# A two-column exponential bias, w_mod ahead of x, one more head group by seven products, another feed-forward order and a search over orders, in an adaLN transformer block

## The chip, the core and the metric

The kernel runs on one core of one Trainium2 chip. The metric is the device time of one execution in microseconds. A core has five engines that each follow an instruction queue of their own: PE (TensorE, matmuls), DVE (VectorE), ACT (ScalarE), POOL (GpSimd) and SP (SyncE, which issues the DMAs here). Engines wait for each other through semaphores. PE writes to PSUM, which has eight banks of 128 x 512 f32; the other tiles lie in SBUF.

## What is computed

```python
def _A_ref(x, k_cache, v_cache, wq, wo):            # 2048 queries, 32 heads of 128, window W = 512 keys
    q = (x @ wq).reshape(B, Sq, Hq, Dh).transpose(0, 2, 1, 3)
    k, v = k_cache[:, :, Sk - W:, :], v_cache[:, :, Sk - W:, :]
    p = softmax(einsum("bhqd,bhkd->bhqk", q, k) * Dh ** -0.5)
    o = einsum("bhqk,bhkd->bhqd", p, v)
    return o.transpose(0, 2, 1, 3).reshape(B, Sq, Hq * Dh) @ wo

def _B_ref(x, w_gate, w_up, w_down):                # Dm 512, Df 1376
    return (gelu(x @ w_gate) * (x @ w_up)) @ w_down

mod = (silu(c) @ w_mod).reshape(1, 6, 1, 512)
sa, ca, ga, sb, cb, gb = (mod[:, i] for i in range(6))
x = x + ga * _A_ref(layernorm(x) * (1 + ca) + sa, ...)
x = x + gb * _B_ref(layernorm(x) * (1 + cb) + sb, ...)
```

Inputs and output are f32.

## The kernel before

**Numbers.** A product of f32 matrices is done with f16 pairs: each operand is split into a high part and the low rest, and three f16 matmuls (high-high, high-low, low-high) add up in one PSUM bank. Names of tiles in the trace: `acc` (16 tiles of 128 x 512) is x and then the residual; `raw` a weight or cache tile as loaded; `A`, `B`, `T`, `S` the split operands of the q product; `k` and `kT` the keys and their transposes; `q`; `p` the exponentials in f32; `pp` their f16 pair; `pT` its transposes by DMA; `oT` the attention output; `st` a small tile with a query block's maxima, biases and sums; `es` a head's scale; `psQ`, `psS`, `psW`, `psO` PSUM banks.

**Attention.** 128 iterations (`NIT`): 16 groups of two heads, each over four query groups of 512. An iteration has two halves, each for 256 queries: PE makes scores into a pair of banks psS (two pairs in turn), DVE takes the row maximum (`s_max`, `st<-psS`), turns it into the bias of the exponential (`st<-st,es`), ACT does two exponentials with that bias (`s_exp`), ACT copies the high part and POOL subtracts for the low part (`pp<-p,pp`), SP transposes both by DMA. Two iterations later PE multiplies by v into psO (one bank), ACT and DVE split the result to oT; three iterations later PE multiplies by wo into psW (two banks) and DVE adds into acc. The next iterations' q goes through psQ (one bank), and ACT and DVE split it. Beside this run the preparations of the next head group (maxima on DVE, scaling and splitting of raw tiles on ACT and POOL), spread over half iterations by `STEPS`.

**q by seven products.** The q products of two heads and two query groups, with the model dimension in two halves, are a 2 x 2 product of blocks. From head group `WINO` on they are made as Strassen and Winograd do: seven products of sums in place of eight (42 matmuls in place of 48), twice for a head group. This needs sums T1 to T4 of h, made once (`t_full`, `t_sum`, `t_split`, on POOL, ACT and DVE), and sums S1 to S4 of each group's weights.

**Feed-forward.** 11 blocks of 128 hidden columns (the last of 96), two halves p of the queries. A unit (p, f) is a block for one half; from block `PLAIN` = 2 on it is made by seven products too (`product`, `stage`), four stages with ACT and DVE behind each (`r`, `hid`), and a queue of down products (`down_put`, `down`) is worked off one after each stage. `UNITS` is the order of the units. `aw_load` and `aw_make` prepare the weights of a later unit; `SPLIT` lists the units that need it (blocks 6 to 9 share their weights between p = 0 and p = 1). The second half's sums (`sums_a`, `sums_b`) are issued at block 4 of the first half.

**Order.** Nothing is issued where it is written. `Weaver` notes every operation with its readers and writers (`note`), ranks the operations back from the end (`rank`), and `issue` plays the program forward against a model of the engines (`play`) and back (`back`), in turns; the best of 8 turns (`TURNS`) is kept up to a point of time, and so on for the points in `CUTS`. Then each engine gets its instructions in the planned order, all from line 418 of the profile. In the plan an operation that `note` marks as `lock` cannot run beside one of POOL: all of POOL's operations, and DVE's tensor_scalar and two-operand operations on SBUF tiles, where they have more than two columns. Where POOL's operation follows closely behind such a one of DVE, an extra wait is put in ("POOL lets DVE in"). The loads ahead of `nc.lead` are issued as written.

**Start.** `PLAN` lists the first steps by name ("stats", "mod", "row", "col" and so on); `mod` is silu(c) @ w_mod for the rows sa and ca (`wm`, four tiles each), and its bound decides the scale of h.

Of the kernel before, what the change touches and what calls it, by code (L numbers as in the profile page):

```python
# [2 lines left out]

# [10 lines left out]
OP = mybir.AluOpType  # L14
# [14 lines left out]
NF = (DFF + P - 1) // P  # L29
# [9 lines left out]
HID = 2.0 ** 38  # L39
HQS = 2.0 ** 9  # L40
QDOWN = 2.0 ** -16
WINO = 3
GATED = 12
ODOWN = 2.0 ** -22
ROUND = 1.0 + 2.0 ** -7
# [34 lines left out]
)  # L80

EARLY = {("wq", 0): (0, 3, 9, 10), ("wq", 1): (0, 3, 10, 11), ("k", 0): (0, 6, 9, 11, 12), ("k", 1): (0, 4, 11, 13, 15),
         ("v", 0): (3, 7, 13, 14), ("wo", 0): (4, 10, 13, 17), ("v", 1): (6, 8, 15, 20), ("wo", 1): (7, 11, 19, 22)}
EARLY_CROSS = (7, 9)
# [2 lines left out]
class Weaver:  # L87
# [1 line left out]

    LAG, DRAIN, LANES, TURNS, SPAN, SHY, EARLY, WORTH = 60.0, 165.0, 8, 8, 3413.0, 1500.0, 40000.0, 5000.0  # L90
    NEAR = 1000.0
    CUTS, BEYOND = (130000.0, 700000.0, 1280000.0, 1400000.0, 1500000.0, None), 25000.0
    NEXT = {"ACT": 95.0, "DVE": 85.0, "POOL": 45.0, "PE": 0.0, "SP": 0.0}

    def __init__(self, nc, tc):
        self.nc, self.tc = nc, tc
        for name, engine in (("vector", "DVE"), ("scalar", "ACT"), ("gpsimd", "POOL"), ("tensor", "PE"), ("sync", "SP")):
            setattr(self, name, self.Port(self, engine, getattr(nc, name)))
        self.joins, self.lead = None, 0
        self.ops, self.held, self.seen, self.before, self.rings, self.table = [], {}, {}, {}, {}, {}  # L100

    class Port:
# [61 lines left out]
    def note(self, engine, what, real, a, k):  # L164
        op = len(self.ops) - bool(self.joins)
        wrote = [x for x in (a[0] if a else k["out"], k.get("accum_out")) if x is not None]
        read = [x for x in list(a[1:]) + list(k.values()) if hasattr(x, "ap") and x is not k.get("accum_out")]
        deps = set()
        n = 1
        for x, write in [(x, False) for x in read] + [(x, True) for x in wrote]:  # L170
            m, lo, hi = self.extent(x)
            n = max(n, m) if engine != "PE" else self.extent(wrote[0])[0]
            key = x.name
            held = self.held.get(key)
            if held is None or write and self.joins:
                continue
            alone = held[:1] == [None]
            if alone:
                lo, hi = -1, 1 << 30
            for e in held:  # L180
                if e and (write or e[3] or alone and self.ops[e[2]][0] != engine) and e[0] < hi and lo < e[1]:
                    deps.add(e[2])
            if write:
                held[:] = [e for e in held if not e or not (lo <= e[0] and e[1] <= hi)]
            held.append((lo, hi, op, write))
            self.seen[key].add(op)
        if what == "activation" and a[2] not in (AF.Copy, AF.Identity):
            for f, s in self.table.items():
                if f != a[2]:
                    deps |= s  # L190
            self.table.setdefault(a[2], set()).add(op)
        deps.discard(op)
        d = (470.0 if what == "dma_start" else 1290.0) if engine == "SP" else self.cost(engine, what, a, k, n, [x.name for x in read])
        if engine == "SP":
            short = what == "dma_start" and any(len(x.ap) > 2 and list(x.ap)[-1][1] <= P for x in a[:2])
            n = 1450.0 if what != "dma_start" else n * 4 * P / (195.0 if short else 390.0)
        flat = [x for x in read if self.extent(x)[0] > 1]
        lock = engine == "POOL" or (engine == "DVE" and not any(x.name.startswith("ps") for x in flat) and n > 2 and
                                    (what == "tensor_scalar" or (len(flat) == 2 and what != "tensor_reduce")))
        if self.joins:  # L200
            self.ops[op][2].update(deps)
        else:
            self.ops.append((engine, d, deps, n, {}))
        self.ops[op][4][engine] = d, lock, real, a, k
# [184 lines left out]
    def done(self, ends, by, until):  # L389

        return sum(1.0 if ends[n] < until else 0.0 for n, e in enumerate(by) if e == "PE" and self.ops[n][3] == N)

    def issue(self):
        at, users = self.rank()
        span, keep, cut = None, {}, 0.0
        for stop in self.CUTS:
            best = None
            for _ in range(self.TURNS):
                order, ends, by, starts = self.play(at, users, span, keep, cut)
                span = max(ends)  # L400
                mark = self.done(ends, by, stop + self.BEYOND) if stop else -span
                if best is None or mark > best[0]:
                    best = mark, order, ends, by, starts
                at = self.back(ends, by, users)
            _, order, ends, by, starts = best
            span = max(ends)
            at = self.back(ends, by, users)
            if stop:
                keep, cut = {n: (starts[n], by[n]) for n in order if starts[n] < stop}, stop
        yields, last = {}, None  # L410
        for n in sorted((n for n in order if self.ops[n][4][by[n]][1]), key=lambda n: starts[n]):
            if by[n] == "POOL" and last is not None and starts[n] < ends[last] + self.NEAR:
                yields[n] = last
            last = n if by[n] == "DVE" else None
        made = {}
        for n in order:
            real, a, k = self.ops[n][4][by[n]][2:]
            made[n] = real(*a, **k)  # L418
            if n in yields:
                self.tc.add_manual_dep(made[n].ins, made[yields[n]].ins.name,  # L420
                                       mybir.DependencyInfo(mybir.DependencyClass.Sync, mybir.DependencyReason.DATA),
                                       reason="POOL lets DVE in")
# [3 lines left out]
def adaln_block(ctx: ExitStack, tc: tile.TileContext, x, k_cache, v_cache, wq, wo,  # L426
# [16 lines left out]
    def small(pool, cols_, bufs=3, name="sm"):  # L443
        return pool.tile([P, cols_], F32, name=name, tag=name, bufs=bufs)
# [116 lines left out]
    def load_mod(j):  # L561
        wm[j] = right.tile([P, NC, D], F32, name="wm", tag="pT", bufs=3)
        for k in range(NC):
            nc.sync.dma_start(wm[j][:, k, :], wmod_r[:, k, j * D:(j + 1) * D])

    def load_x(qg):
        for t in range(4 * qg, 4 * qg + 4):
            nc.sync.dma_start(acc[t], x[t * P:(t + 1) * P, :])
# [4 lines left out]
    def load_raw(kind, h):  # L573
# [9 lines left out]
            nc.sync.dma_start(t, wo[h * DH:(h + 1) * DH, :])  # L583
        RAW[kind, h] = t

    load_x(0)
    load_x(1)
    load_mod(1)
    load_mod(0)
    load_raw("k", 0)  # L590
    load_raw("wq", 0)
    load_x(2)
    load_raw("wq", 1)
    load_raw("k", 1)
    load_x(3)
    load_raw("v", 0)
    load_raw("wo", 0)
    load_raw("v", 1)
    load_raw("wo", 1)
    nc.lead = len(nc.ops)  # L600


    e = small(base, NC, 1, "sil")
    nc.scalar.activation(e, csb, AF.Exp, scale=-1.0)
    nc.vector.tensor_scalar_add(e, e, 1.0)
# [2 lines left out]
    spread = right.tile([P, NC, D], F32, name="spread", tag="pT", bufs=3)  # L608
    for k in range(NC):
        nc.vector.tensor_scalar_mul(spread[:, 0, k * P:(k + 1) * P], ones, silu[:, k:k + 1])  # L610


    KINDS = ("wq", "k", "v", "wo")
# [218 lines left out]
    def s_max(it, b):  # L832
        if b == 0:
            ST[it] = small(right, 12, 5, "st")
        st = ST[it]
        nc.vector.tensor_reduce(st[:, 2 * b:2 * b + 2], PSS[it, b], op=OP.max, axis=AX.X, negate=True)
        for n in (2 * b, 2 * b + 1):
            nc.vector.tensor_scalar(st[:, n:n + 1], st[:, n:n + 1], ES[head_qg(it)[0]][:, 0:1], LOG_PS,
                                    op0=OP.mult, op1=OP.add)

    def s_exp(it, b):
        st = ST[it]
# [174 lines left out]
    for half, name, *a in PLAN:  # L1017
        if name == "chunk":
            a[3:] = [ENG[e] for e in a[3:]]
        if half < 0:  # L1020
            STEP[name](*a)
        else:
            at(half, STEP[name], *a)

# [33 lines left out]

    for p in range(2):
        for c in range(2):  # L1060
            n = 8 + 7 * (2 * p + c)
            at(n, t_full, p, c, "11", Y)
            at(n, t_full, p, c, "12", Y)
            at(n + 1, t_sum, p, c, "11", "12", "11")
# [368 lines left out]
    def aw_load(u):  # L1433
        ff_load(u[1], u)
# [166 lines left out]
    for c, (a, b, d) in enumerate(((15.5, 15, 16.25), (15, 16.25, 16.5), (16.5, 16, 17.25), (16, 17.25, 17.5))):  # L1601
        at(e + a, ln2_chunk, 0, c)
        at(e + b, ln2_high, 0, c)
        at(e + d, ln2_low, 0, c, nc.gpsimd)
    UNITS = [(0, f) for f in range(PLAIN, 6)] + [(p, f) for f in range(6, NF - 1) for p in range(2)] + \
        [(0, NF - 1)] + [(1, f) for f in range(6)] + [(1, NF - 1)]
    SPLIT = [u for u in UNITS if not (u[0] and 6 <= u[1] < NF - 1)]
    at(e + 10, aw_load, UNITS[0])
    at(e + 11, aw_load, UNITS[1])
# [81 lines left out]
    for n, u in enumerate(UNITS):  # L1691
        p, f = u
        k = SPLIT.index(u) if u in SPLIT else None
        if k is not None:
            if k + 4 < len(SPLIT):
                aw_load(SPLIT[k + 4])
            if k + 2 < len(SPLIT):
                aw_make(SPLIT[k + 2])
        if WDS:
            w = WDS.pop(0)  # L1700
            wd_load(w)
# [58 lines left out]
```

## Time and profile before

| | us |
|---|---|
| median of 3 runs | 1678.78 (1678.69 to 1679.83) |
| the profiled execution | 1676.12 |
| its span in the trace | 1674.3 |
| first f16 matmul | 26.42 |
| first scores, first product with v | 31.96, 52.01 |
| last matmul ends | 1669.9 |

The profiled execution is one of its own; the trace gives its span, and the 1.8 us between span and time lie around it. All instructions of the weave have line 418 (L418), so a row is told by its engine and its tiles: `DVE TENSOR_SCALAR st<-st,es` is the bias. In a row of the timeline the two numbers ahead are the start and the length in us, and the square brackets hold the idle time before it and what ended that. In a row of the grouped view the numbers behind the first bar are the busy time in us and the mean of one in ns, behind the second the idle time before. The granted TensorE clock was 0.998 of full speed on the mean.

### The profile page before, as it was taken

The page shows a single profiled execution, that of the slowest core. Times are in us where ns is not written, and L with a number is a line of the kernel's source. Part 1 is how long each engine was busy: PE and PEld are TensorE (multiplying, and loading weights), DVE is VectorE, ACT ScalarE, POOL GpSimd, SP SyncE. Part 2 cuts the span into 40 slices and gives each one's busy share as a digit, 9 for nine tenths or more (in the row PEclk, how much of TensorE's full clock was granted, in tenths as well). Part 3 has the DMA queues.
Part 4 walks back from the last instruction along what each step waited for, and adds up shares of the span by engine and source line. Part 5 has one row for each costly group of instructions (what it writes and reads, how often), then busy time and mean ns, then how long its engine had stood idle before and what let it go on. Part 6 is the DMA issues. An engine that isn't in the chain of part 4 may idle for free.

```text
span 1674.3 us, 24105 instructions
## 1 busy us (share of the span) xinstructions
PE 1659.9 (99%) x7750; PEld 764.6 (46%) x7750; DVE 1267.5 (76%) x2371; ACT 1216.4 (73%) x2412; POOL 1238.5 (74%) x1027
## 2 busy tenths in 40 slices
PE   8999999999999999999999999999999999999999
PEld 5444444444444444444444444444444444444444
DVE  7877777778787878777898888778787956565555
ACT  5877787877777777778787878787787976554441
POOL 3878898868675867676676889999777898855530
PEclk9999999999999999999999999999999999999999
DMA  8778568877777778786889887879777612011111
GB/s 239 141 137 157 108 126 167 182 138 161 138 148 124 145 121 150 127 146 128 168 191 182 173 161 157 158 153 194 136 133 151 116 37 63 23 49 33 31 42 51
DMA packets 666350, 217.10 MB, mean 130 GB/s; under 512 B 581552, under 2 KB 648112, under 8 KB 666224
## 3 DMA queue, kind: packets, MB, share of 16 engines
q1 hardware_dynamic: 666224, 215.57, 64.7%
q8 instruction: 61, 1.00, 0.2%
q14 instruction: 65, 0.53, 0.1%
HBM read 68.68 MB, written 4.19 MB: 44 GB/s over the span
## 4 chain that ended last, share of the span: by engine, by line
PE 94%; DVE 3%; DMA 1%; ACT 1%; POOL 1%; issue 0%; SPq 0%; DVEq 0%; POOLq 0%; ACTq 0%
PE psS L418 31%; PE psW L418 24%; PE psO L418 22%; PE psQ L418 18%; DVE st L418 0%; DVE acc L418 0%; DMA raw<-in_A_wq_dram 0%; DMA wm<-in_w_mod_dram 0%; DVE mx L418 0%; SPq L418 0%; DVE bnst L418 0%; DVE h L418 0%; DVE r L418 0%; POOL T L418 0%; DVE hid L418 0%
## 5 line engine op out<-in xcount | busy, mean ns | idle before, releaser
L418 POOL TENSOR_TENSOR pp<-p,pp 128x1024 f16<-128x1024 f32 x256 | 545.3, 2130 | 250.0 <-ACT pp L418 151.1
L418 ACT ACTIVATE p<-psS,st,es 128x512 f32<-128x512 f32 x512 | 393.2, 774 | 168.7 <-DVE st L418 167.5
L418 DVE SCALAR_TENSOR_TENSOR acc<-psW,st,acc 128x512 f32<-128x512 f32 x496 | 368.2, 743 | 116.0 <-PE psW L418 115.0
L418 PE MATMUL psW<-wo,oT 128*128 128x512 f16 x1536 | 415.0, 379 | 0.0
L418 PE MATMUL psS<-kT,q 128*128 128x512 f16 x1536 | 384.2, 379 | 0.3 <-DVE q L418 0.2
L418 PE MATMUL psO<-pT,v 128*128 128x512 f16 x1536 | 373.9, 379 | 0.1
L418 DVE TENSOR_REDUCE st<-psS 128x2 f32<-128x1024 f32 x256 | 312.9, 1222 | 63.1 <-PE psS L418 62.2
L418 ACT ACTIVATE pp<-p 128x1024 f16<-128x1024 f32 x256 | 271.4, 1060 | 3.8
L418 PEld LDWEIGHTS <-v 128*128 128x128 f16 x1536 | 150.1, 98 | 180.9 <-issue 0.8
L418 PEld LDWEIGHTS <-oT 128*128 128x128 f16 x1536 | 150.3, 98 | 180.3
L418 PEld LDWEIGHTS <-q 128*128 128x128 f16 x1536 | 147.5, 98 | 171.6 <-issue 1.1
L418 ACT ACTIVATE oT<-psO 128x512 f16<-128x512 f32 x128 | 76.3, 596 | 92.1 <-PE psO L418 91.6
L418 PEld LDWEIGHTS <-aw 128*128 128x128 f16 (+1 forms) x840 | 84.2, 100 | 100.8 <-issue 5.2
L418 PE MATMUL psQ<-B,A 128*128 128x512 f16 x528 | 128.7, 379 | 0.0
L418 DVE SCALAR_TENSOR_TENSOR oT<-psO,oT 128x512 f16<-128x512 f32 x128 | 88.4, 690 | 39.6 <-ACT oT L418 39.6
L418 PE MATMUL psS<-T,aw 128*128 128x512 f16 (+1 forms) x480 | 115.8, 379 | 0.6 <-POOL T L418 0.6
L418 PEld LDWEIGHTS <-A 128*128 128x128 f16 x756 | 74.4, 98 | 90.0 <-issue 2.2
L418 PE MATMUL psQ<-T,S 128*128 128x512 f16 x468 | 113.9, 379 | 0.0
L418 ACT ACTIVATION_READ_ACCUMULATOR p<-psS,st,es 128x1 f32 x512 | 101.9, 199 | 0.0
L418 DVE TENSOR_TENSOR r<-psS,h 128x512 f32<-128x512 f32 (+1 forms) x60 | 40.8, 688 | 73.8 <-PE psS L418 44.5
L418 PEld LDWEIGHTS <-S 128*128 128x128 f16 x624 | 61.1, 98 | 73.6
L418 DVE TENSOR_REDUCE mx<-raw 128x1 f32<-128x512 f32 x128 | 85.8, 675 | 6.4 <-DMA raw<-in_A_k_cache_dram 5.1
(210 smaller groups left out, 2263.5 us busy)
## 6 DMA issues: line engine op xcount, KB each, us to landing
raw<-in_A_k_cache_dram SPq DMA_DIRECT2D x32, 256.0 KB, 3.9
raw<-in_A_wq_dram SPq DMA_DIRECT2D x32, 256.0 KB, 3.3
raw<-in_A_v_cache_dram SPq DMA_DIRECT2D x32, 256.0 KB, 3.2
raw<-in_A_wo_dram SPq DMA_DIRECT2D x32, 256.0 KB, 3.0
pT<-pp SPq DMA_TRANSPOSE x512, 3.2
raw<-in_B_w_gate_dram SPq DMA_DIRECT2D x24, 256.0 KB, 3.1
raw<-in_B_w_up_dram SPq DMA_DIRECT2D x24, 256.0 KB, 3.2
raw<-in_B_w_down_dram SPq DMA_DIRECT2D x20, 256.0 KB, 3.0
```

What stands on the lines that cost most here:

```text
L418: made[n] = real(*a, **k)
```

## The change

Five edits. The bias of a half's two exponentials is one operation on two columns of `st`, not one for each column. The loads start with the four parts of w_mod's second row, and x follows in four parts with other loads between; what the modulation needs (`HURRY`, and silu) is put first in every rank. `WINO` is 2 in place of 3, and the T tiles' steps start earlier and closer together. `UNITS` takes blocks 6 and 7 of the first half ahead of those of the second, and `MAKE` moves the weights' steps accordingly. In `issue`, after the 8 turns, up to 32 more plays with randomly shifted ranks are tried for each of nine stretches, and the best is kept.

```diff
-WINO = 3
+WINO = 2
...
+HURRY = ("mod", "row", "col", "cols_add", "cols_bound", "cols_scale")
...
-    CUTS, BEYOND = (130000.0, 700000.0, 1280000.0, 1400000.0, 1500000.0, None), 25000.0
+    CUTS, BEYOND, FAR = ((60000.0, 16), (130000.0, 16), (700000.0, 4), (1280000.0, 4), (1340000.0, 32), (1400000.0, 32), (1450000.0, 32),
+                         (1500000.0, 16), (None, 0)), 25000.0, (300.0, 1000.0, 3000.0)
...
+        if self.hurry and not self.joins:
+            self.first.append(op)
...
+    def rush(self, at):
+        for n in self.first:
+            at[n] = -1e8 + n
+        return at
...
-        for stop in self.CUTS:
+        draw = random.Random(7)
+        for stop, shakes in self.CUTS:
             best = None
-            for _ in range(self.TURNS):
+            for turn in range(self.TURNS + shakes):
+                if turn >= self.TURNS:
+                    far = draw.choice(self.FAR)
+                    at = [x + draw.uniform(-far, far) for x in best[5]]
                 order, ends, by, starts = self.play(at, users, span, keep, cut)
...
+    load_mod(1)
     load_x(0)
-    load_x(1)
-    load_mod(1)
     load_mod(0)
     load_raw("k", 0)
     load_raw("wq", 0)
-    load_x(2)
+    load_x(1)
     load_raw("wq", 1)
     load_raw("k", 1)
-    load_x(3)
+    load_x(2)
     load_raw("v", 0)
     load_raw("wo", 0)
     load_raw("v", 1)
     load_raw("wo", 1)
+    load_x(3)
...
-        for n in (2 * b, 2 * b + 1):
-            nc.vector.tensor_scalar(st[:, n:n + 1], st[:, n:n + 1], ES[head_qg(it)[0]][:, 0:1], LOG_PS,
-                                    op0=OP.mult, op1=OP.add)
+        s = st[:, 2 * b:2 * b + 2]
+        nc.vector.tensor_scalar(s, s, ES[head_qg(it)[0]][:, 0:1], LOG_PS, op0=OP.mult, op1=OP.add)
...
-            n = 8 + 7 * (2 * p + c)
+            n = 6 + 4 * (2 * p + c)
...
-    UNITS = [(0, f) for f in range(PLAIN, 6)] + [(p, f) for f in range(6, NF - 1) for p in range(2)] + \
+    UNITS = [(0, f) for f in range(PLAIN, 8)] + [(1, 6), (1, 7)] + [(p, f) for f in range(8, NF - 1) for p in range(2)] + \
         [(0, NF - 1)] + [(1, f) for f in range(6)] + [(1, NF - 1)]
+    MAKE = {(0, 7): None, (1, 7): 7, (0, 8): 8, (0, 9): 9, (0, 10): 10}
...
         k = SPLIT.index(u) if u in SPLIT else None
+        k = MAKE.get(u, None if k is None else k + 2)
         if k is not None:
-            if k + 4 < len(SPLIT):
-                aw_load(SPLIT[k + 4])
             if k + 2 < len(SPLIT):
-                aw_make(SPLIT[k + 2])
+                aw_load(SPLIT[k + 2])
+            if k < len(SPLIT):
+                aw_make(SPLIT[k])
```

How it moves instructions, at three places. First DVE in the middle of attention, one iteration of a head (`st` the maxima and biases, `acc` and `oT` as above; the rows say operation, output, inputs, shape). Before:

```order
L418 TENSOR_REDUCE st<-psS 128x2
L418 SCALAR_TENSOR_TENSOR acc_74<-psW,st,acc_74 128x512
L418 TENSOR_SCALAR st<-st,es 128x1 x2
L418 SCALAR_TENSOR_TENSOR acc_75<-psW,st,acc_75 128x512
L418 TENSOR_REDUCE st<-psS 128x2
L418 TENSOR_SCALAR st<-st,es 128x1 x2
L418 SCALAR_TENSOR_TENSOR oT<-psO,oT 128x512
L418 SCALAR_TENSOR_TENSOR acc_76<-psW,st,acc_76 128x512
```

and with the change:

```order
L436 TENSOR_REDUCE st<-psS 128x2
L436 SCALAR_TENSOR_TENSOR acc_74<-psW,st,acc_74 128x512
L436 TENSOR_SCALAR st<-st,es 128x2
L436 SCALAR_TENSOR_TENSOR acc_75<-psW,st,acc_75 128x512
L436 TENSOR_REDUCE st<-psS 128x2
L436 TENSOR_SCALAR st<-st,es 128x2
L436 SCALAR_TENSOR_TENSOR oT<-psO,oT 128x512
L436 SCALAR_TENSOR_TENSOR acc_76<-psW,st,acc_76 128x512
```

Nothing has moved there; two one-column operations have become one of two columns, and the same additions stand behind it.

Second the loads at the start of SP's queue (`acc` is x, `wm` w_mod). Before:

```order
L418 DMA acc_76<-in_A_x_dram 128x512
L418 DMA acc_77<-in_A_x_dram 128x512
L418 DMA wm<-in_w_mod_dram 128x512 x8
L418 DMA raw<-in_A_k_cache_dram 128x4x128
L418 DMA raw<-in_A_wq_dram 128x4x128
```

(with acc_70 to acc_75 ahead), and with the change:

```order
L436 DMA wm<-in_w_mod_dram 128x512 x4
L436 DMA acc_70<-in_A_x_dram 128x512
L436 DMA acc_71<-in_A_x_dram 128x512
L436 DMA acc_72<-in_A_x_dram 128x512
L436 DMA acc_73<-in_A_x_dram 128x512
L436 DMA wm<-in_w_mod_dram 128x512 x4
L436 DMA raw<-in_A_k_cache_dram 128x4x128
L436 DMA raw<-in_A_wq_dram 128x4x128
L436 DMA acc_74<-in_A_x_dram 128x512
```

The first k and wq stand behind 12 loads of x and w_mod, where there were 16, and the first x behind four parts of w_mod.

Third POOL in the feed-forward part, at the last of the second half's T tiles (`T4`, from `ft` and `hf`, the sums; `aw` are a later unit's weights; numbers tell the tiles apart). Before:

```order
L418 TENSOR_TENSOR ft_3108<-B21_0_3040 128x512
L418 TENSOR_TENSOR aw_3127<-S1f_3123,aw_3127 128x256
L418 TENSOR_TENSOR ft_3108<-ft_3108,hf_3078 128x512
L418 TENSOR_TENSOR aw_3127<-S2f_3124,aw_3127 128x256
L418 TENSOR_TENSOR S1f_3144<-raw_3094 128x256
L418 TENSOR_TENSOR T4_0_3075<-ft_3108,T4_0_3075 128x512
```

and with the change:

```order
L436 TENSOR_TENSOR ft_3116<-B21_0_3048 128x512
L436 TENSOR_TENSOR ft_3116<-ft_3116,hf_3086 128x512
L436 TENSOR_TENSOR aw_3156<-S2f_3153,aw_3156 128x256
L436 TENSOR_TENSOR T4_0_3083<-ft_3116,T4_0_3083 128x512
L436 TENSOR_TENSOR aw_3156<-S1f_3152,aw_3156 128x256
```

The last T4 has 120 rows of POOL behind it before and 110 with the change, while two units of the first half, not one, stand ahead of the second half's first unit. Over the whole program PE has 7450 f16 matmuls of 128 x 512 in place of 7462, DVE 253 operations fewer, ACT 14 more, POOL 5 more, and SP as many as before.

More of the change, by code (lines that the diff above doesn't have):

```diff
@@ L1 @@
 import math
+import random
 from contextlib import ExitStack
@@ L98, in __init__ @@
             setattr(self, name, self.Port(self, engine, getattr(nc, name)))
-        self.joins, self.lead = None, 0
+        self.joins, self.lead, self.hurry, self.first = None, 0, False, []
         self.ops, self.held, self.seen, self.before, self.rings, self.table = [], {}, {}, {}, {}, {}
@@ L391, in done @@
         return sum(1.0 if ends[n] < until else 0.0 for n, e in enumerate(by) if e == "PE" and self.ops[n][3] == N)
+    def rush(self, at):
+        for n in self.first:
+            at[n] = -1e8 + n
+        return at
     def issue(self):
         at, users = self.rank()
+        at = self.rush(at)
         span, keep, cut = None, {}, 0.0
-        for stop in self.CUTS:
+        draw = random.Random(7)
+        for stop, shakes in self.CUTS:
             best = None
-            for _ in range(self.TURNS):
+            for turn in range(self.TURNS + shakes):
+                if turn >= self.TURNS:
+                    far = draw.choice(self.FAR)
+                    at = [x + draw.uniform(-far, far) for x in best[5]]
                 order, ends, by, starts = self.play(at, users, span, keep, cut)
-                span = max(ends)
-                mark = self.done(ends, by, stop + self.BEYOND) if stop else -span
+                if turn < self.TURNS:
+                    span = max(ends)
+                mark = self.done(ends, by, stop + self.BEYOND) if stop else -max(ends)
                 if best is None or mark > best[0]:
-                    best = mark, order, ends, by, starts
-                at = self.back(ends, by, users)
-            _, order, ends, by, starts = best
+                    best = mark, order, ends, by, starts, at
+                if turn < self.TURNS:
+                    at = self.rush(self.back(ends, by, users))
+            _, order, ends, by, starts, at = best
             span = max(ends)
-            at = self.back(ends, by, users)
             if stop:
                 keep, cut = {n: (starts[n], by[n]) for n in order if starts[n] < stop}, stop
+            at = self.rush(self.back(ends, by, users))
         yields, last = {}, None
@@ L599, in adaln_block @@
     load_raw("wo", 1)
+    load_x(3)
     nc.lead = len(nc.ops)
+    nc.hurry = True
     e = small(base, NC, 1, "sil")
@@ L610, in adaln_block @@
         nc.vector.tensor_scalar_mul(spread[:, 0, k * P:(k + 1) * P], ones, silu[:, k:k + 1])
+    nc.hurry = False
     KINDS = ("wq", "k", "v", "wo")
@@ L1020, in adaln_block @@
         if half < 0:
+            nc.hurry = name in HURRY
             STEP[name](*a)
+            nc.hurry = False
         else:
```

## The prediction

> **What bounds the kernel now.** I read the page first, then the busy time by stretch, then the chain of waits.
>
> ```profile
> PE 1659.9 (99%) x7750; PEld 764.6 (46%) x7750; DVE 1267.5 (76%) x2371; ACT 1216.4 (73%) x2412; POOL 1238.5 (74%) x1027
> PE 94%; DVE 3%; DMA 1%; ACT 1%; POOL 1%; issue 0%; SPq 0%; DVEq 0%; POOLq 0%; ACTq 0%
> 60.00:1300.00 1240.00, 1240.00 (x5773) 562.46 (x5773) 987.46 (x1901) 970.27 (x1955) 977.62 (x719) 1.00 0.78 150
> 250.85 2.59 PE psQ L418 x12
> ```
>
> The first two lines say that PE is busy for 99% of the span and owns 94% of the chain that ends last. The third, the stretch from 60 to 1300 us (columns: length, then busy time of PE, PEld, DVE, ACT, POOL, then clock, DMA share, GB/s), says more: in 1240 us of attention PE has no gap at all, at a full granted clock. So two kinds of edit can gain here: fewer matmuls (the fourth line, a piece of the chain, gives 2.59/12 = 0.216 us for one 128x512 f16 matmul), or the holes outside this stretch. DVE is busy for 987.46/1240 = 79.6% and POOL for 78.8% of it. They are covers, not bounds, and they are not thick: whoever adds work or waits to DVE spends a fifth of its time at most.
>
> **The bias of the exponentials: 512 one-column operations become 256 two-column ones.** Saved is an instruction per half iteration, 84.7/512 = 0.165 us of DVE, 42 us in all; beside a PE without gaps that is worth nothing. What matters is how the two-column form behaves. No row shows it on this tile, but two rows show it on others:
>
> ```profile
> L418 DVE TENSOR_SCALAR st<-st,es 128x1 f32<-128x1 f32 x512 | 84.7, 206 | 3.9
> L418 DVE TENSOR_SCALAR ffs<-av 128x2 f32<-128x2 f32 x1 | 0.8, 814 | 0.0
> L418 DVE TENSOR_SCALAR ffs<-av 128x1 f32<-128x1 f32 x1 | 0.1, 144 | 0.0
> L418 DVE TENSOR_SCALAR cols<-cols,ffs 128x8 f32<-128x8 f32 x1 | 1.0, 1031 | 0.0
> L418 DVE TENSOR_SCALAR cols<-cols,sc 128x8 f32<-128x8 f32 x1 | 0.2, 224 | 0.0
> 1247.84 1.16 POOL L418 TENSOR_TENSOR v<-raw,v 128x512 f16<-128x512 f32 x1
> 1248.21 0.81 DVE L418 TENSOR_SCALAR ffs<-av 128x2 f32<-128x2 f32 x1
> 1277.85 1.16 POOL L418 TENSOR_TENSOR v<-raw,v 128x512 f16<-128x512 f32 x1
> 1278.00 1.03 DVE L418 TENSOR_SCALAR cols<-cols,ffs 128x8 f32<-128x8 f32 x1
> 188.07 1.27 POOL L418 TENSOR_TENSOR tf<-tf 128x512 f32<-128x512 f32 x1
> 188.26 0.32 DVE L418 TENSOR_SCALAR st<-st,es 128x1 f32<-128x1 f32 x2
> ```
>
> A scale of two columns took 0.814 us where the same scale of one column took 0.144; one of eight columns took 1.031 us in one place and 0.224 in another. The timeline tells why: both long ones began while POOL was inside an operation, and both ended with it (1248.21 + 0.81 = 1249.02 against 1247.84 + 1.16 = 1249.00; 1279.03 against 1279.01). The last two rows are the control: two one-column biases ran 0.19 us into a POOL operation of 1.27 us and were done in 0.32 us. So on this trace a short DVE operation on an even number of SBUF columns waits for POOL's running operation to end, and a single column doesn't. The waits were 0.814 - 0.144 = 0.67 and 1.031 - 0.224 = 0.81 us, mean 0.74.
>
> [...]
>
> What is the wait worth? The rows are:
>
> ```profile
> L418 POOL TENSOR_TENSOR pp<-p,pp 128x1024 f16<-128x1024 f32 x256 | 545.3, 2130 | 250.0 <-ACT pp L418 151.1
> 702.14 0.32 DVE L418 TENSOR_SCALAR st<-st,es 128x1 f32<-128x1 f32 x2
> 702.46 0.78 ACT L418 ACTIVATE p<-psS,st,es 128x512 f32<-128x512 f32 x1 [2.31 <-DVE st L418]
> 702.73 1.46 PE L418 MATMUL psS<-kT,q 128*128 128x512 f16 x6
> 707.91 1.46 PE L418 MATMUL psS<-kT,q 128*128 128x512 f16 x6
> L418 DVE SCALAR_TENSOR_TENSOR acc<-psW,st,acc 128x512 f32<-128x512 f32 x496 | 368.2, 743 | 116.0 <-PE psW L418 115.0
> ```
>
> A half iteration is 707.91 - 702.73 = 5.18 us of PE. Per half DVE gains 0.165 us and loses 0.74 on average, 0.57 net: 0.57/5.18 = 11 points, from 79.6% to about 91%. The mean still fits into DVE's idle time of 20.4% x 5.18 = 1.06 us per half; the long waits don't. POOL's commonest operation, pp, takes 2.13 us and fills 545.3 us of some 1300 of attention, 42% of the time. A bias that falls into it at random waits longer than 1.06 us in half of the cases, by 0.53 us on average: 256 x 0.42 x 0.5 x 0.53 = **28 us** of lateness that no idle time takes in. Queued behind the bias on DVE are the additions to acc that free the two psW banks, the oT and q products that free psO and psQ (one bank each), and PE waits for all of them; ACT's exponentials wait directly (2.31 us at 702.46), but psS has two pairs, so they have a whole half of room. Against the 28 us stands that DVE often waits for PE before acc (115 us over 496 additions), so not every late bias makes a late bank. I take half, **+14 us**. Bounds: 0 (everything hidden; a gain is excluded, since PE has no gap in this stretch for a faster DVE to close) and 28 us plus what DVE does not catch up. If nothing hid the net loss at all, it would be 0.57 x 256 = 146 us; PE's banks and DVE's idle time speak against that.
>
> [...]
>
> **Seven products one head group sooner.** Head group 2 has two such products, and each goes from 48 to 42 matmuls. 12 x 0.216 = **-2.6 us**, straight off a PE without gaps. By the order the kernel issues 14 more operations on ACT and 5 more on POOL for it and for what moved between them, and the T tiles must be made in half the iterations:
>
> ```profile
> POOL 3878898868675867676676889999777898855530
> 124.00:172.00 48.00, 48.00 (x224) 21.80 (x223) 37.85 (x71) 35.73 (x73) 42.92 (x31) 1.00 0.79 150
> ```
>
> POOL's tenths in 40 slices of 41.9 us reach 8 early on, and from 124 to 172 us it is busy for 42.92/48 = 89%. With the steps moved forward POOL comes near 100% there. What is late next is the first product of group 2, and the pp that keep POOL busy. Between 0 and 3 us; I take 0, nearer to the row, which still has 11% free.
>
> **The feed-forward order.** The second half's T tiles are the one hole behind attention:
>
> ```profile
> 1453.85 1.16 POOL L418 TENSOR_TENSOR T<-ft,T 128x512 f16<-128x512 f32 x1 [0.69 <-DVE hid L418]
> 1456.17 0.59 PE L418 MATMUL psS<-T,aw 128*128 128x512 f16 x2 [0.55 <-POOL T L418]
> 1458.18 1.46 PE L418 MATMUL psS<-B,aw 128*128 128x512 f16 x6 [1.41 <-DVE r L418]
> 1460.35 1.17 POOL L418 TENSOR_TENSOR T<-ft,T 128x512 f16<-128x512 f32 x1
> 1463.78 0.81 PE L418 MATMUL psS<-B,aw 128*128 128x512 f16 x3 [1.56 <-ACT r L418]
> 1473.21 0.81 PE L418 MATMUL psS<-B,aw 128*128 128x512 f16 x3 [0.21 <-ACT r L418]
> ```
>
> PE's waits are 0.55 + 1.41 + 1.56 + 0.21 = 3.73 us. The first is for the T tile itself; the others for DVE and ACT, which finish a product's r while no down product stands between. After the change two units of the first half stand ahead of the second half's first unit in place of one, 42 matmuls = 9.1 us more and the down products between them, and in the order shown above POOL writes its last T4 ten rows earlier, counted from its end. So the 0.55 goes, and most of the waits on r, which come from units that follow each other bare. The stretch without down products stays, though, so I leave 1 us: **-2.7 us**, bounds -3.7 and 0.
>
> **The loads.** Before:
>
> ```profile
> 1.23 3.81 SPq L418 DMA_DIRECT2D acc<-in_A_x_dram  x8
> 5.09 4.86 SPq L418 DMA_DIRECT2D wm<-in_w_mod_dram  x8
> 16.52 1.48 DVE L418 TENSOR_REDUCE mx<-raw 128x1 f32<-128x512 f32 x2 [5.12 <-DMA raw<-in_A_k_cache_dram]
> 22.82 0.72 ACT L418 ACTIVATE k<-raw,av 128x512 f16<-128x512 f32 x1 [1.88 <-DVE sc L418]
> 31.96 1.90 PE L418 MATMUL psS<-kT,q 128*128 128x512 f16 x8
> 52.01 1.24 PE L418 MATMUL psO<-pT,v 128*128 128x512 f16 x5
> ```
>
> k and wq stand behind 16 loads on SP; now they stand behind 12. Eight loads take 3.8 to 4.9 us of issue, so four fewer bring k some 2 us forward, out of a DVE wait of 5.12 us. But x(0) now lands behind four parts of w_mod, so its statistics, which DVE did before that wait, move into it. The first score at 31.96 us also hangs on h of x(0), so one gain meets one loss: 0, bounds -3 and +2 us. What would be late next is DVE, busy without a break from the statistics to the first q.
>
> **The order search** moves instructions by up to 3 us in plan. Within 60 to 1300 us it has no gap to win: 0. Its loss lies in the bias term, since it plans the two-column form as cheap.
>
> **Sum.** -2.6 - 2.7 + 14 + 0 + 0 + 0 = +8.7 us on the profiled 1676.12 us, 1684.8. That execution lies 2.66 us under the median of the three runs, 1678.78; carried to it, the forecast is **1687.5 us**, 0.5% slower.
>
> **The rivals.** 0.2%, 3.4 us here, is about what a measurement of this kernel can tell from no change.
>
> *Faster: the waits are hidden.* The blocked biases fall into DVE's 1.06 us per half, and two banks of psW and two pairs of psS take in the rest. For it: the mean net loss of 0.57 us is half of the idle time, and PE's gaps are nil today with DVE at 80%. Against it: pp alone makes waits up to 2.13 us. Then the other terms are left, -5.3: 1673.5 us; with a good head 1670. The same comes out if the one row of two columns was chance. It is decided where PE's new waits stay under 5.3 - 3.4 = 1.9 us in all. Chance 0.27.
>
> *Mostly hidden*: 2 to 8.7 us of waits eat the gains: 1675.4 to 1682.1 us. Chance 0.20.
>
> *DVE becomes the bound.* If the whole 28 us reach PE, 1678.78 - 5.3 + 28 = 1701.5 us; this is decided where DVE passes about 95% over many halves. For it: one slice of the page shows DVE at 9 tenths already. Chance 0.13.
>
> *The change doesn't do what it says.* The hole at 1456 to 1473 us stays since r, not T, ends three of its four waits (-2.6 only), and the T tiles cost 3 us at POOL: -2.6 + 14 + 3 = +14.4, 1693 us. Chance 0.10.
>
> *The forecast*, with 8.7 to 21.5 us of new waits against the 5.3 of gains: 1682.1 to 1695 us. Chance 0.30.
>
> **The numbers.** Slower by over 0.2%: 0.30 + 0.10 + 0.13 = 0.53; within: 0.20; faster: 0.27. The faster case and the others lie on both sides, so the range goes from 1671 us (the faster case nearly whole) to 1704 us (the whole 28 us and 2.5 more); the forecast's own range is 1682 to 1695.
>
> **What would show it.** The group of st<-st,es should stand as 128x2 x256 with a mean near 0.9 us, its rows ending with POOL's; DVE busy near 91% from 60 to 1300 us with PE's busy share there under 100%, and PE's idle named by DVE acc, oT or mr. If the mean is near 0.2 us, the rule from the two rows was wrong and the faster case holds. Also 7450 big matmuls in place of 7462; PE's first wait for a T tile of the second half gone; the first score within 3 us of 31.96. I am wrong on the size if the group is long and PE's row from 60 to 1300 us still reads 100%.

## The result and the profile after

| | before | with the change |
|---|---|---|
| median, us | 1678.69 (5 runs, 1676.18 to 1679.83) | 1719.49 (5 runs, 1716.81 to 1725.83) |
| ratio | 1 | 1.0256, 95% interval 1.0233 to 1.0280 |
| span of the profiled execution, us | 1674.3 | 1716.3 |

The change makes the kernel 41 us slower. The forecast had the direction and the mechanism, and far too small a size: 1687.5 us, with a range that ended at 1704. All medians and ratios here are of executions at the usual speed; of the six of `e6_ff` below, two are left out for that, one of 10069.91 us (the profiled one) and one of 1748.88 us.

The same views of the changed kernel: the page's busy times and its chain by engine, the stretch from 60 to 1300 us, and the group of the bias.

```profile
PE 1669.4 (97%) x7738; PEld 760.0 (44%) x7738; DVE 1415.0 (82%) x2118; ACT 1223.1 (71%) x2426; POOL 1247.3 (73%) x1032
PE 38%; DVE 25%; ACT 7%; issue 5%; POOL 4%; DMA 2%; SPq 0%; ACTq 0%; DVEq 0%; POOLq 0%
60.00:1300.00 1240.00, 1207.92 (x5568) 539.58 (x5567) 1090.21 (x1606) 947.71 (x1910) 945.32 (x696) 1.00 0.75 145
L436 DVE TENSOR_SCALAR st<-st,es 128x2 f32<-128x2 f32 x256 | 261.0, 1019 | 2.8
```

PE, which had no gap in this stretch, is idle for 1240 - 1207.92 = 32 us of it. (It starts 5568 instructions in place of 5773; at 0.216 us these 205 are 44 us. The busy time of a train of matmuls goes to its modelled end, so short gaps read shorter than they are; the count is nearer to the loss.) PE's share of the chain has fallen from 94% to 38%, and DVE, which is busy for only 87.9% of the stretch, owns 25%. The 256 two-column biases take 261.0 us where the 512 one-column ones took 84.7. One of them takes 1.019 us on the mean, where one of a single column took 0.206 (the second number behind the bar of its row); 228 of the 256 end within 60 ns behind the end of a POOL operation. Before, 495 of the 512 of one column began while POOL was inside an operation, and none took over 0.216 us. The timeline shows how it goes on from there:

```profile
708.52 2.13 POOL L436 TENSOR_TENSOR pp<-p,pp 128x1024 f16<-128x1024 f32 x1 [2.37 <-issue]
709.41 1.26 DVE L436 TENSOR_SCALAR st<-st,es 128x2 f32<-128x2 f32 x1
710.59 0.68 DVE L436 SCALAR_TENSOR_TENSOR oT<-psO,oT 128x512 f16<-128x512 f32 x1
710.77 0.78 ACT L436 ACTIVATE p<-psS,st,es 128x512 f32<-128x512 f32 x1 [1.37 <-DVE st L436]
711.32 0.08 PEld L436 LDWEIGHTS psO<-ident,mx 128*8 128x8 f32 x1 [0.28 <-DVE oT L436]
713.16 0.27 DVE L436 TENSOR_REDUCE mr<-psO 8x1 bf16<-8x128 f32 x1
713.49 1.46 PE L436 MATMUL psO<-pT,v 128*128 128x512 f16 x6 [0.55 <-DVE mr L436]
```

POOL's pp runs until 710.65 and the bias until 710.67. Behind it on DVE stands oT, which empties psO; PE wants that bank for the maxima of the next head group (mx), and its weight load (row PEld) waits 0.28 us. DVE then reduces these maxima out of the same bank to mr, behind two more additions to acc and two operations more, and PE waits 0.55 us for that. PE's waits by what ended them, over the whole span (the sum in us, how often, the longest):

```profile
PE psO L436 <- DVE oT L436: 12.9, 15, 1.6
PE psO L436 <- DVE mr L436: 10.0, 19, 0.6
PE psW L436 <- DVE acc L436: 5.1, 11, 1.1
```

The first two, 23 us together, are waits in psO, the only bank of its kind, most of them at the crosses, where it serves mx and mr between two products with v (11.5 of the 12.9 us stand at the product for mx, all of the 10.0 at the product with v behind mr). They are the largest of the view.

### The profile page after: what moved, and what is told of

Same layout as the page of the kernel before. It is cut to its first block, busy times and chain, and to the rows that moved or that the text cites. A ratio compares the mean times of both kernels' runs of the same rounds, so it can differ in the third digit from the quotient of the medians.

```text
span 1716.3 us, 23853 instructions
## 1 busy us (share of the span) xinstructions
PE 1669.4 (97%) x7738; PEld 760.0 (44%) x7738; DVE 1415.0 (82%) x2118; ACT 1223.1 (71%) x2426; POOL 1247.3 (73%) x1032
## 4 chain that ended last, share of the span: by engine, by line
PE 38%; DVE 25%; ACT 7%; issue 5%; POOL 4%; DMA 2%; SPq 0%; ACTq 0%; DVEq 0%; POOLq 0%
PE psS L436 16%; DVE st L436 13%; PE psW L436 9%; PE psO L436 8%; DVE acc L436 6%; PE psQ L436 5%; ACT p L436 3%; DVE mx L436 2%; DVE h L436 1%; DVE oT L436 1%; DMA raw<-in_A_v_cache_dram 1%; POOL pp L436 1%; ACT pp L436 1%; ACT raw L436 1%; DVE q L436 1%
## 5 line engine op out<-in xcount | busy, mean ns | idle before, releaser
L436 DVE SCALAR_TENSOR_TENSOR acc<-psW,st,acc 128x512 f32<-128x512 f32 x496 | 364.1, 736 | 42.7 <-PE psW L436 42.3
L436 DVE TENSOR_SCALAR st<-st,es 128x2 f32<-128x2 f32 x256 | 261.0, 1019 | 2.8
L436 PE MATMUL psQ<-T,S 128*128 128x512 f16 x504 | 123.0, 379 | 0.0
L436 PE MATMUL psQ<-B,A 128*128 128x512 f16 x480 | 119.5, 382 | 0.8 <-DVE q L436 0.7
L436 PEld LDWEIGHTS <-A 128*128 128x128 f16 x696 | 68.4, 98 | 86.0 <-issue 5.9
L436 PEld LDWEIGHTS <-S 128*128 128x128 f16 x672 | 65.7, 98 | 79.5 <-issue 0.7
L436 POOL TENSOR_TENSOR q<-h,q 128x512 f16<-128x512 f32 x84 | 97.4, 1160 | 1.4 <-ACT q L436 1.4
```

## The experiments

Each ran beside the kernel before on the same chip; the ratios are to that. Its median lay between 1676.65 and 1677.32 us in these batches.

**The bias alone, taken out and put in.** `e1_onecol` is the change with the old bias:

```diff
-        s = st[:, 2 * b:2 * b + 2]
-        nc.vector.tensor_scalar(s, s, ES[head_qg(it)[0]][:, 0:1], LOG_PS, op0=OP.mult, op1=OP.add)
+        for n in (2 * b, 2 * b + 1):
+            nc.vector.tensor_scalar(st[:, n:n + 1], st[:, n:n + 1], ES[head_qg(it)[0]][:, 0:1], LOG_PS,
+                                    op0=OP.mult, op1=OP.add)
```

> The change with the bias as two one-column operations again, all else kept. If the whole loss is the two-column bias waiting for POOL: the bias group reads 0.16 to 0.21 us a piece, PE is busy for 1240 of 1240 us between 60 and 1300 us, and the time is before's 1678.7 less the gains of the other parts, 5.3 us by the sum: 1673 us (1670 to 1679). If a part of the loss comes from the searched order, the loads or the T tiles: the bias group is short as well, but the time stays above 1682 us.

`e2_twocol` is the kernel before with the opposite edit.

> The kernel before with the two-column bias alone. If the wait for POOL is the whole loss: the bias takes 0.9 to 1.1 us on the mean, DVE is busy for 88 to 91% between 60 and 1300 us, and the time is the change's 1719.5 plus the 5.3 us that the other parts should gain: 1720 to 1728 us. If the loss needs the new order as well: under 1710 us.

Measured: 1673.36 us, ratio 0.9977 (0.9969 to 0.9986), and 1724.40 us, ratio 1.0283 (1.0269 to 1.0297). Their biases and their stretches from 60 to 1300 us, first of e1, then of e2:

```profile
L436 DVE TENSOR_SCALAR st<-st,es 128x1 f32<-128x1 f32 x512 | 85.0, 206 | 2.9
60.00:1300.00 1240.00, 1239.29 (x5769) 562.04 (x5768) 983.94 (x1903) 982.58 (x1975) 979.16 (x719) 1.00 0.79 150
```

```profile
L418 DVE TENSOR_SCALAR st<-st,es 128x2 f32<-128x2 f32 x256 | 253.2, 989 | 4.2
60.00:1300.00 1240.00, 1209.77 (x5579) 542.82 (x5578) 1082.81 (x1601) 948.70 (x1901) 933.30 (x680) 1.00 0.73 144
```

One edit of two lines moves PE between a full and a 97.6% busy stretch, in either program (5579 instructions in place of 5769). It is worth 1719.49 - 1673.36 = 46 us in the one and 1724.40 - 1676.70 = 48 us in the other; the other four parts of the change together gain 3.9 us (0.0023 x 1676.7).

**How long POOL's operations are.** In `e9_split`, POOL makes the low part of the exponentials in two operations.

```diff
-        nc.gpsimd.tensor_tensor(pp[:, :, 1, :], p32, pp[:, :, 0, :], op=OP.subtract)
+        for j in range(2):
+            nc.gpsimd.tensor_tensor(pp[:, j, 1, :], p32[:, j, :], pp[:, j, 0, :], op=OP.subtract)
```

> The change with the low part of the exponentials made by two POOL operations of 512 columns in place of one of 1024, so that POOL's longest operation is 1.16 us, not 2.13. If the bias waits for the rest of POOL's running operation: its mean falls from 1.02 to about 0.6 us and its longest from 2.7 to under 2, and at least half of the 46 us of loss comes back: under 1700 us, though POOL does some 40 us more. If the two-column form is slow in itself: its mean stays at 1.0 us and the time at 1715 us or more.

Measured: 1695.73 us, ratio 1.0108 (1.0093 to 1.0123), 24 less than the change. The groups of the bias and of pp, then one bias with the five POOL operations that it met:

```profile
L436 DVE TENSOR_SCALAR st<-st,es 128x2 f32<-128x2 f32 x256 | 173.0, 676 | 2.9
L436 POOL TENSOR_TENSOR pp<-p,pp 128x512 f16<-128x512 f32 x512 | 582.1, 1158 | 253.3 <-issue 134.3 <-ACT pp L436 92.5 <-POOL q L436 8.5
176.10 5.39 DVE L436 TENSOR_SCALAR st<-st,es 128x2 f32<-128x2 f32 x1
175.64 1.27 POOL L436 TENSOR_TENSOR tf<-tf 128x512 f32<-128x512 f32 x1
176.87 1.16 POOL L436 TENSOR_TENSOR T<-tf,T 128x512 f16<-128x512 f32 x1
177.98 1.27 POOL L436 TENSOR_TENSOR tf<-tf 128x512 f32<-128x512 f32 x1
179.20 1.16 POOL L436 TENSOR_TENSOR A<-raw,A 128x512 f16<-128x512 f32 x1
180.32 1.15 POOL L436 TENSOR_TENSOR tf<-B 128x512 f32<-128x512 f16 x1
```

The bias falls from 1.019 to 0.676 us, though POOL does more. So its length follows that of POOL's operations, and half of the loss goes with it. The longest should have come under 2 us and didn't: 7 of the 256 took over 1.23 us, where 87 had, but the six longest of them took 2.9 to 5.4. Most biases get in at the first end of a POOL operation (208 here, 218 in the change), even where the next POOL operation follows at once. Some don't: 22 here and 12 in the change ran on through at least one more, as the rows from 176.10 us show, where the bias ends with the fifth. What decides it, no run shows.

**Even or odd columns.** `e10_three` makes one operation on three columns, the third a zero; the planner is told that it is free of POOL.

```diff
-        nc.vector.tensor_reduce(st[:, 2 * b:2 * b + 2], PSS[it, b], op=OP.max, axis=AX.X, negate=True)
-        s = st[:, 2 * b:2 * b + 2]
-        nc.vector.tensor_scalar(s, s, ES[head_qg(it)[0]][:, 0:1], LOG_PS, op0=OP.mult, op1=OP.add)
+        r = it % 5
+        nc.vector.tensor_reduce(bi[:, 6 * r + 3 * b:6 * r + 3 * b + 2], PSS[it, b], op=OP.max, axis=AX.X, negate=True)
+        nc.vector.tensor_scalar(st[:, 3 * b:3 * b + 3], bi[:, 6 * r + 3 * b:6 * r + 3 * b + 3],
+                                ES[head_qg(it)[0]][:, 0:1], LOG_PS, op0=OP.mult, op1=OP.add)
```

> The change with the bias as one operation on three columns (the third is a zero that nothing reads), which the planner is told to take as free of POOL. If only an even number of columns waits for POOL: the bias takes about 0.2 us and the time is as with two one-column operations, 1673 us (1670 to 1677). If any number above one waits: the bias takes 1 us and the time is 1715 to 1725 us.

Measured: 1734.98 us, ratio 1.0343 (1.0328 to 1.0359).

```profile
L436 DVE TENSOR_SCALAR st<-bi,es 128x3 f32<-128x3 f32 x256 | 234.8, 917 | 3.5
```

Three columns wait as two do: one such operation took 0.917 us on the mean, where one on two columns took 1.019. The prediction's "even number of SBUF columns" was wrong; in this case one column never waits (no tensor_scalar of one column took over 0.267 us in the traces of before and of the change), and two, three and eight do (eight: 1.031 us in one meeting, in the trace of before). What sets one column apart, no run shows. Why this kernel is 15 us slower still than the change, with a shorter mean wait, is open; the run was forecast at 1725 us at most.

**A plan that knows.** `e3_lock` lets the planner mark operations of two columns as `lock`, so that in the plan they cannot run beside one of POOL.

```diff
-        lock = engine == "POOL" or (engine == "DVE" and not any(x.name.startswith("ps") for x in flat) and n > 2 and
+        lock = engine == "POOL" or (engine == "DVE" and not any(x.name.startswith("ps") for x in flat) and n > 1 and
```

> The change with the planner's rule at more than 1 column in place of more than 2, so that the plan keeps the bias off POOL's operations and lets POOL wait for it. If the loss is only a plan that did not know of the wait: 1675 to 1690 us. If a plan cannot remove it, since the bias comes ready when the scores do and POOL is busy for four fifths of the time: the wait moves in part to POOL, the bias still takes 0.5 us or more, and the time is between 1695 and 1725 us.

Measured: 1683.75 us, ratio 1.0039 (1.0026 to 1.0053).

```profile
L436 DVE TENSOR_SCALAR st<-st,es 128x2 f32<-128x2 f32 x256 | 104.6, 413 | 0.6
60.00:1300.00 1240.00, 1235.32 (x5740) 558.69 (x5739) 986.54 (x1654) 971.17 (x1950) 985.36 (x727) 1.00 0.76 149
POOL q L436 <- DVE st L436: 6.7, 19, 0.8
```

With the same work in another order, 167 of 256 biases take under 0.3 us (42 in the change), and 36 of the 46 us are back. The plan doesn't cover the waits but avoids most of them. The mark also brings the extra waits of POOL for DVE: POOL waits 34.3 us for `st` in 89 places (the last line is one group of them), so order and extra waits aren't told apart. The plan loses 10 us against e1 and gains nothing by the second operation saved.

**Which bank.** `e4_cross` gives the crosses a psW bank.

```diff
-        pt = bank("psO") if pt is None else pt
+        pt = bank("psW", 2) if pt is None else pt
```

(in `cross_a` and `cross_b`)

> The change with the crosses of the maxima (mx, mr, iv) in a psW bank in place of psO. PE waited 12.9 us in psO for oT and 10.0 us for mr. If the single bank psO is what hands DVE's lateness on to PE: these two waits fall under 5 us together and the time to about 1700 us (1695 to 1708). If DVE's lateness reaches PE by whichever bank comes next: the waits turn up at acc and psW, and the time stays within 8 us of 1719.5.

Measured: 1738.49 us, ratio 1.0361 (1.0345 to 1.0377), outside both ranges. PE's waits:

```profile
PE psW L436 <- DVE acc L436: 33.9, 45, 2.5
PE psO L436 <- DVE oT L436: 1.4, 1, 1.4
```

The waits for oT are nearly gone and those for acc have risen from 5.1 to 33.9 us: in these two kernels DVE's lateness reaches PE by the bank that the crosses use, and psW feeds four additions per iteration. The single bank psO was the place, not the cause. Not all of the 19 us over the change are waits: the granted clock of the profiled execution was 0.991 on the mean, against 0.998, and by my estimate 0.007 x 1737 = 12 us go with it. Why the clock was lower is open.

**Why so much of it reaches PE.** `e12_work` adds one maximum over 512 columns to each half iteration of the kernel before (the real one overwrites it), `e13_unplanned` the same with a duration of nothing in the plan.

```diff
+        nc.vector.tensor_reduce(st[:, 2 * b:2 * b + 1], PSS[it, b][:, 0, :], op=OP.max, axis=AX.X, negate=True)
         nc.vector.tensor_reduce(st[:, 2 * b:2 * b + 2], PSS[it, b], op=OP.max, axis=AX.X, negate=True)
...
+        if engine == "DVE" and what == "tensor_reduce" and n == N and a[0].name.startswith("st"):
+            return 1.0
```

> The kernel before with one more maximum on DVE in each half iteration, over 512 columns of the scores, ahead of the real one, which overwrites it; the planner counts it. It adds some 0.65 us of DVE per half, nearly what the two-column bias adds net (1.02 - 0.33 = 0.69), but even and known to the plan, and it waits for nothing of POOL. If DVE's added time as such makes the loss: 1715 to 1730 us. If the unevenness of the waits or the plan's not knowing of them does: 1677 to 1695 us.

> The same added maximum, but the planner takes its duration as nothing, as it takes the bias's wait as nothing. If the plan's not knowing makes the loss: 1705 to 1730 us, well above the run with the planned one. If the unevenness does (long waits of 1.2 to 2.1 us): both stay under 1695 us.

Measured: 1680.35 us, ratio 1.0020 (1.0011 to 1.0030), and 1700.96 us, ratio 1.0140 (1.0123 to 1.0157). The added group and the stretch, first planned, then unplanned:

```profile
L418 DVE TENSOR_REDUCE st<-psS 128x1 f32<-128x512 f32 x256 | 176.0, 688 | 50.5 <-PE psS L418 49.5
60.00:1300.00 1240.00, 1239.69 (x5771) 561.63 (x5769) 1121.04 (x2142) 982.40 (x1948) 983.44 (x726) 1.00 0.77 150
```

```profile
L420 DVE TENSOR_REDUCE st<-psS 128x1 f32<-128x512 f32 x256 | 174.6, 682 | 37.2 <-PE psS L420 36.6
60.00:1300.00 1240.00, 1230.78 (x5713) 555.96 (x5711) 1110.69 (x2117) 975.89 (x1949) 958.30 (x699) 1.00 0.76 148
```

176 us of extra DVE work is what the two-column bias cost (261.0 - 84.7 = 176; in e2 it is 168.5). Even and planned, it brings DVE to 1121.04/1240 = 90.4% and costs PE 0.3 us in this stretch (2 instructions of 5773) and the kernel 1680.35 - 1676.65 = 3.7 us; by the profiled executions, 3.1 us are lost in the last 1700 matmuls. Even and unplanned, it costs the kernel 24 us, between the two ranges that were expected. Uneven and unplanned, as in e2, 48 us.

In the stretch itself the distance is larger. PE starts 2 instructions fewer than before in e12, 60 in e13 and 194 in e2; at 0.216 us these are 0.4, 13 and 42 us. (Of the rest of e13's 24 us, 4.4 are lost by the 200th matmul and 6.5 in the last 1700, most of these in one wait of 4.4 us for a weight tile wd.) So a plan that doesn't know of the added time makes under a third of the loss in the stretch. The larger part needs what e13 lacks: waits of 0 to 3.9 us in place of an even 0.68, at the bias and not ahead of the maximum, set by POOL. Which of these it is wasn't tried, nor uneven waits that the plan knows.

**The other parts, each alone on the kernel before.** `e5_wino` is `WINO = 2` with the new T steps, `e6_ff` and its repetition `e6b_ff` (made for its profile) the order of units with `MAKE`, `e7_loads` the loads with `HURRY`, `e8_search` the new `issue` loop with `CUTS` and `FAR`; their diffs are the parts of the change's diff of those names. `e11_both` is e5 and e6 together.

> The kernel before with head group 2 by seven products and the T tiles' steps moved forward, nothing else. If PE's work alone counts: 12 matmuls of 0.216 us less, -2.6 us. If the T tiles press POOL: between -2.6 and +1 us, with a wait of PE for T near the start of group 2.

> The kernel before with the new order of feed-forward units and of their weights alone. If the hole at 1456 to 1473 us comes from units that follow each other bare: it shrinks from 3.7 to about 1 us, -2.7 us. If it only moves to where the down products run out: within 1 us of before.

> The kernel before with the feed-forward order alone, once more for its profile. The time as in the run before it, 5 to 6 us under the kernel before. If the gain lies in the hole, PE's waits between 1455 and 1475 us are gone (3.7 us) and the remaining 2 us show as shorter runs of products beside it; if it lies elsewhere, the distance from the first feed-forward unit to the last matmul is as before and the rest of the program is shorter.

> The kernel before with the loads of w_mod first and the modulation first in rank, alone. If k and wq a few us earlier are made up by x(0) later: within 1 us of before, first scores within 1 us of 31.96. If the head gains: -1 to -2 us and the first product with v before 51 us.

> The kernel before with the longer search over orders alone. If the search wins nothing on the chip: within 2 us of before. If it explains why the change without the two-column bias gained 3.3 us where its parts alone give 7.6: +4 us.

> The kernel before with the feed-forward order and seven products for head group 2 together, without the new loads, the search and the two-column bias. If the parts add up: 6.4 + 1.5 us under before, about 1669 us, and faster than both kernels. If the T tiles and the new order cost each other something: 1671 to 1673 us.

| part alone | median, us | ratio, 95% interval |
|---|---|---|
| e5_wino | 1675.76 | 0.9991 (0.9982 to 0.9999) |
| e6_ff | 1670.79 | 0.9962 (0.9949 to 0.9975) |
| e6b_ff | 1670.81 | 0.9960 (0.9945 to 0.9976) |
| e7_loads | 1677.61 | 1.0002 (0.9994 to 1.0011) |
| e8_search | 1676.30 | 0.9996 (0.9987 to 1.0005) |
| e11_both | 1671.26 | 0.9964 (0.9951 to 0.9976) |

The feed-forward order is the part that gains, 6.5 us by e6b; its stretch from 1400 to 1500 us, against the same stretch of before:

```profile
1400.00:1500.00 100.00, 99.59 (x464) 45.35 (x463) 63.89 (x86) 52.95 (x100) 78.16 (x84) 1.00 0.15 41
```

```profile
1400.00:1500.00 100.00, 96.27 (x449) 43.87 (x448) 62.25 (x83) 54.28 (x102) 74.45 (x80) 1.00 0.16 43
```

PE's idle time falls from 3.7 to 0.4 us there, and the distance from the 1000th to the 900th last matmul by 3.8 us. Seven products for group 2 gain 1.5 us alone and nothing on top of this. The 12 matmuls are gone in e11 as well; but its last 1700 matmuls, the end of attention and the whole feed-forward part, take 2.5 us longer than those of e6b, though the feed-forward code is the same. In e1 the last 1700 matmuls are 3.0 us longer than in e6b. Why the plan comes out worse there wasn't tried. e6 and e11 beat both kernels; the two can't be told apart.

## Why the prediction was right in kind and wrong in size

**The wait** was right: two-column biases end with a POOL operation (228 of the 256 in the change), taking them away (e1) took the whole loss away, putting them in alone (e2) made all of it, and the rivals in which they were hidden fall. The mean wait was 1.019 - 0.206 = 0.81 us, not 0.74; that two meetings sized it so well was luck, since both were with operations of 1.16 us and the most frequent one, pp, takes 2.13.

**The step that failed is "I take half, +14 us. Bounds: 0 ... and 28 us plus what DVE does not catch up".** It measured 46 us. Three things in it were wrong. First, a bias was to fall into a pp at random, with a chance of 0.42. In the trace of the change 203 of the 256 began while pp ran, 79%. Counted bias by bias, what the waits have above 1.06 us adds up to 39.8 us, not 28. Second, half of that was to be hidden; the measured loss is larger than all of it. Third, DVE's idle time of 1.06 us per half was taken as if it absorbed any wait below that. e12 shows that it can, for a delay that the plan knows: 90.4% busy, no loss in the stretch. e13 shows that it cannot, for one of 0.68 us that the plan doesn't know: 13 us in the stretch, with no wait above 1.06 us at all. So the lateness counted above 1.06 us was no bound: in the change the loss is 46 us against 39.8, in e2 48 against 33.6, in e9 22 (1695.73 - 1673.36) against 14.4, nearly all of it from the six longest biases.

**"It plans the two-column form as cheap"** got no price of its own in the forecast. e3 puts it at 36 of 46 us, by a plan that keeps most biases off POOL's operations and makes POOL wait in places.

**"DVE becomes the bound"** came nearest in time but not in kind: DVE is busy for 87.9% of the stretch, under the 95% that it named, and e12 is busier without loss in the stretch. By PE's waits, what bounds is the chain through the bias, DVE's next operations and a bank, at single places.

**Where PE waits.** The working spoke of acc, oT and q, the list of signs of acc, oT or mr; it was above all oT and mr in psO, 23 us. The signs were right, but the crosses were not in the sum. But e4 shows that the place alone explains nothing.

**The other terms.** Seven products, -2.6: -1.5 alone (-3.0 to -0.2), nothing beside the new feed-forward order. The feed-forward order, -2.7 with a bound of -3.7: -6.5 in the medians and -5.1 between the two profiled executions, of which 3.8 stand in the hole; the other 1.3 are shared out in pieces under 1 us. The 1 us left for the stretch without down products was not needed. The loads, 0: +0.3 (-1.0 to +1.8); in the changed kernel the first scores stand at 31.31 us, within the 3 us forecast. The search, 0: -0.7 (-2.2 to +0.8). The T tiles at POOL, 0: PE's waits for POOL's T in psQ add up to 0.3 us in the change and 1.1 us in e1. The four together were forecast as -5.3 and measured as -3.9 (-5.2 to -2.3).

## What to carry to other kernels

Where a plan fixes the order of engines in advance, don't price an operation that turns out slower by the engine's mean idle time: here the same added work cost 3.7 us known to the plan, 24 us unknown, and 48 us unknown and uneven. Price it as unplanned, then ask what the same plan makes of it when told. Before two small operations become one, look in the trace for the same operation in the wider form beside a busy neighbour, and count how often its end falls on the neighbour's end. In these runs an idle share of a tenth covered even work that the plan knew (e12, 9.6% idle in the stretch from 60 to 1300 us: 3.7 us lost), and not the delays that it didn't know (e13, 10.4%: 24 us).

## What the runs showed that was not expected

In these runs a tensor_scalar of DVE between SBUF tiles on three columns waits for POOL like one on two (0.917 and 1.019 us on the mean, against 0.206 for a single column), and now and then one on two lets several POOL operations go ahead, one behind the other (22 of 256 in e9, 12 in the change): 5.4 us in the longest case of e9. And DVE at 90.4% beside a PE without gaps costs almost nothing (a ratio of 1.0020), where 87.9% with uneven waits that the plan doesn't know costs 44 us in the stretch from 60 to 1300 us, by the count of PE's instructions.
